# A state-space model and a dilated local attention on one core: the attention weights transposed by two DMAs instead of by TensorE

## The chip, the cores and the metric

The kernel runs on 1 core of one Trainium2 chip. The metric is the device time of one execution in microseconds (us), lower is better; the time before is the median of three runs. The engines are called TensorE (PE in the profile), VectorE (DVE), ScalarE (ACT), GpSimd (POOL) and SyncE (SP); SP issues nearly all DMAs of this kernel from one queue.

## The reference

Two layers over a sequence of 2048 rows of 448 values, joined along the last axis. Part A is a diagonal complex state-space model (448 states), a skip term added. Part B is attention with 16 heads of 28, in which each position sees itself and seven earlier ones, two steps apart (the eight taps).

```python
def A(x, ...):                       # x: 1 x 2048 x 448
    Lam_bar = exp(dt * Lam)          # dt = exp(log_dt)
    Bu = einsum("bld,pd->blp", x, ((Lam_bar - 1) / Lam)[:, None] * Bmat)
    for t in range(L):
        h = Lam_bar * h + Bu[:, t]
        hs.append(h)
    return 2 * einsum("blp,dp->bld", stack(hs, 1), Cmat).real + x * Dskip

def B(x, wqkv, wo):                  # H = 16, Dh = 28, W = 8, dil = 2
    q, k, v = split(x @ wqkv)
    idx = pos[:, None] - 2 * arange(8)[None, :]      # masked where idx < 0
    logits = einsum("bhsd,bhswd->bhsw", q, k[idx]) * Dh ** -0.5
    attn = softmax(where(idx >= 0, logits, -1e9), axis=-1)
    o = einsum("bhsw,bhswd->bhsd", attn, v[idx])
    return o.reshape(B, S, D) @ wo
```

## The kernel before

The sequence is cut into 128 chunks of 16 positions. A chunk is a partition (or a column, where a tensor is transposed), and the position in the chunk, j = 0 to 15, is a loop. Positions are taken in two halves (b = 1: j 8 to 15; b = 0: j 0 to 7) and each half in two groups of four (r = 1, 0; g = 2b + r).

**Units and their order.** Each piece of work is a unit, added to a planner (`P.add`) with its engine, its function and what it depends on. A unit's number is the order in which it was added. The list `ORDER` says in which order the units are issued; each engine, and each DMA queue, works through its own part of it strictly in turn, so an instruction that waits holds back all that stand behind it on the same engine. Where a unit may run on ScalarE or on VectorE (evictions of PSUM and a few copies), 1000 added to its number means VectorE. PSUM is given out as one double bank ("W") and six single ones ("s"); a unit that needs one waits until an eviction has released it.

**Projections (0 to 45 us).** SP loads x transposed by DMA (`load(j)`, L362), four positions to a group. TensorE forms q, k (L477, L484, L510) and v (L756, L763); ScalarE and VectorE evict them (L215 to L221, the helper `copy`). Units 46, 47 and 48 (`cx.double`, L450) copy 64 rows of the x of positions 8 to 11, 4 to 7 and 0 to 3 into the other 64, for matmuls of 64 rows (`rr`); each must wait for the four loads of its group.

**Logits.** `prod` (L650, L652, L656) multiplies q with shifted k on VectorE, two taps at a time (tp = 3, 2, 1, 0); products of tp 1 and 0 carry 1024 further elements (the last 64 feature rows, of two other taps). `summ` (L667, L673) sums over the features of a head with selector matmuls into the logits tile: its partitions are (i, r, h), the position in its group, the group and the head; its columns are eight rows, one for each tap, of the 128 chunks.

**Softmax.** `softmax(b)` adds eight units: mask; the maximum over the taps on VectorE (`top`, L696); its subtraction by matmul (`sub`, L700); the exponential on ScalarE (`exp`, L706); the sum by matmul (`tot`, L711); reciprocal and product on VectorE (`norm`, L715, L717), which leave the weights `attn_t` in the shape of the logits; eight transposes on TensorE into PSUM (`tr`, L723), one for each tap, after which a chunk is a partition; and two copies on ScalarE into `attn` (`ev`, L728), which reorder them for the value products. Units 206 to 213 are these for b = 1, 214 to 221 for b = 0.

**Values and output of part B.** `pv` multiplies the weights with the values on VectorE (`mul`, L818: 3584 elements, two taps by four positions) and sums (L821, L830, L833). The sums are transposed by DMA (`trd`, L858) or, for the last group, on TensorE (L870), then go through the output weights (L886, L894, L901), are evicted and stored (L911). `halo` copies values from the chunk before (L776, L777).

**Part A.** B and C are loaded; C is transposed by one DMA (L1010) and first used by the y matmuls. `scan` runs, for seven blocks of states m, a chain of matmuls and ScalarE evictions with powers of the state matrix that VectorE builds (`powers`, L1183). `outputs` forms y from the states (L1431, L1435), and stores it (L1450).

Of the kernel before, what the change touches and what calls it, by code (L numbers as in the profile page):

```python
# [88 lines left out]
def act(n):  # L89
    return n / 1200.0 + 0.055  # L90
# [115 lines left out]
class Ctx:  # L206
# [41 lines left out]
    def consts2(self):  # L248
# [22 lines left out]
        def masks():  # L271
            G.memset(mrow[:], 0.0)
            G.affine_select(out=mrow[:], in_=mrow[:], compare_op=ALU.not_equal, fill=-1e9,
                            base=-3, pattern=[[1, 4]], channel_multiplier=1)
            G.memset(mcol[:], 1.0)
            for b in range(2):
                for k in range(2):
# [39 lines left out]
class PartB:  # L317
# [372 lines left out]
    def softmax(self, b, prio):  # L690
# [29 lines left out]
        def tr():  # L720
            pt = box["pt"] = self.psum.tile([NCH, W, 2, 4, H], bf16, name="pt_at", tag="s")
            for w in range(W):
                nc.tensor.transpose(pt[:, w].rearrange("q r i h -> q i r h"), box["a"][:, w, :], cx.ident[:])  # L723
# [848 lines left out]
```

## Time and profile before

| | |
|---|---|
| median of three runs | 139.52 us (139.02 to 140.0) |
| the profiled execution | 138.77 us |
| its span, first to last instruction | 137.1 us |
| granted TensorE clock | 1.000 |
| busy, share of the span: TensorE | 130.8 us, 95% |
| VectorE | 124.1 us, 91% |
| ScalarE | 89.9 us, 66% |
| GpSimd | 17.3 us, 13% |

The profile shows one execution. A busy TensorE is not TensorE at its peak: matmuls overlap, and their ends are modelled. A group line reads: code line, engine, operation, output<-input with shapes, count, then busy us, mean ns of one, and the engine's idle time ahead of them with what ended it. A timeline line begins with its start and its length; a line with SPq shows SP issuing a DMA. The chain of waits follows the last instruction back to what released it, step by step. A row by stage gives a window, its width, and for PE, PEld (weight loads), DVE, ACT and POOL the busy time with the number of instructions; then the clock, the DMA engines' busy share and GB/s.

### The profile page before, as it was taken

To read this page: it belongs to the slowest core of one execution; us is meant where nothing else is said; L and a number is where in the kernel's file an instruction comes from. 1 tells how busy PE (TensorE), PEld (TensorE's weight loads), DVE (VectorE), ACT (ScalarE), POOL (GpSimd) and SP (SyncE) were. 2 spreads that over 40 slices of the span, in tenths; PEclk is the share of its full clock that TensorE was granted. 3 is DMA by queue.
4 is the path that set the end of the run, shared out by engine and by line. 5 is a ranking of instruction groups with operands and counts; after the bars stand their busy time and mean duration, and the time that the engine had idled before them with its cause. 6 is when DMAs were issued, how large, how long until landed. Compare 5 with 4: busy or idle time off the path is not lost.

```text
span 137.1 us, 2853 instructions
## 1 busy us (share of the span) xinstructions
PE 130.8 (95%) x1078; PEld 68.1 (50%) x1085; DVE 124.1 (91%) x136; ACT 89.9 (66%) x202; POOL 17.3 (13%) x69
## 2 busy tenths in 40 slices
PE   5999999999999999999999999999999999999990
PEld 1534334444556453756534663554665555445750
DVE  2369999899999999999999999999999999999950
ACT  3555588998553977856685999987737252463571
POOL 7589800028000000000000000000000000000000
PEclk9999999999999999999999999999999999999999
DMA  4988944554643938835899009600000464917654
GB/s 130 263 135 199 190 88 60 153 117 112 82 100 67 104 69 134 154 77 154 235 155 244 6 0 106 200 0 2 0 5 0 120 148 42 245 49 237 197 167 140
DMA packets 39582, 16.05 MB, mean 117 GB/s; under 512 B 31573, under 2 KB 38932, under 8 KB 39569
## 3 DMA queue, kind: packets, MB, share of 16 engines
q1 hardware_dynamic: 39506, 15.87, 54.5%
q8 instruction: 8, 0.13, 0.4%
q14 instruction: 5, 0.04, 0.1%
q10 hardware_dynamic: 63, 0.01, 0.0%
HBM read 4.32 MB, written 3.67 MB: 58 GB/s over the span
## 4 chain that ended last, share of the span: by engine, by line
PE 81%; SPq 10%; ACT 3%; DMA 2%; issue 1%; ACTq 0%
PE y_ps L1435 16%; PE v_ps L763 7%; SPq L362 6%; PE qk_ps L477 6%; PE scb L1233 6%; PE wo_ps L894 5%; PE scp L1233 5%; PE logits L667 4%; DMA rb<-in_B_x_dram 2%; PE wo_ps L901 2%; PE scb L1292 2%; PE scP L1233 2%; PE scb L1257 2%; PE y_ps L1431 2%; PE v_ps L756 2%
## 5 line engine op out<-in xcount | busy, mean ns | idle before, releaser
L818 DVE TENSOR_TENSOR prods<-attn,vd 128x3584 bf16<-128x3584 bf16 x12 | 24.0, 2017 | 0.0
L821 DVE TENSOR_TENSOR rb<-rb,prods 128x3584 bf16<-128x3584 bf16 x11 | 22.2, 2019 | 0.1
L652 DVE TENSOR_TENSOR prods<-qk 128x3072 bf16<-128x3072 bf16 (+1 forms) x15 | 19.1, 1325 | 0.0
L1435 PE MATMUL y_ps<-Ccat,qk 128*128 128x448 bf16 x60 | 15.1, 352 | 0.1
L477 PE MATMUL qk_ps<-rb 128*128 128x512 bf16 x60 | 14.4, 379 | 0.5 <-DMA rb<-in_B_x_dram 0.3
L215 ACT CAST qk<-wo_ps 128x448 bf16<-128x448 f32 (+1 forms) x16 | 8.2, 528 | 10.1 <-PE wo_ps L894 6.5
L215 ACT CAST vd<-v_ps 128x448 bf16<-128x448 f32 x15 | 7.4, 539 | 5.8 <-PE v_ps L763 4.5
L1435 PE MATMUL y_ps<-Ccat,h 128*128 128x448 bf16 x45 | 11.0, 353 | 0.0
L1233 PE MATMUL scb<-xaT_sb,Bcat 128*128 128x512 bf16 x42 | 10.9, 380 | 0.0
L1233 PEld LDWEIGHTS <-Bcat 128*128 128x128 bf16 x84 | 7.6, 100 | 6.6 <-issue 0.4
L1285 ACT CAST ubuf<-scb 128x64 bf16<-128x64 f32 x35 | 7.1, 218 | 5.6 <-PE scb L1292 3.5
L763 PE MATMUL v_ps<-rb 128*128 128x448 bf16 x48 | 9.9, 353 | 0.0
L217 ACT ACTIVATE qk<-qk_ps 64x512 bf16<-64x512 f32 (+1 forms) x15 | 8.9, 599 | 0.9 <-PE qk_ps L484 0.4
L656 DVE TENSOR_TENSOR prods<-qk 128x768 bf16<-128x768 bf16 (+3 forms) x18 | 9.1, 565 | 0.3 <-ACT qk L215 0.2
L477 PEld LDWEIGHTS <-rb 128*128 128x128 bf16 x60 | 5.6, 98 | 7.6 <-issue 0.7
L1435 PEld LDWEIGHTS <-qk 128*128 128x128 bf16 x60 | 5.9, 98 | 5.3
L818 DVE TENSOR_TENSOR rb<-attn,vd 128x3584 bf16<-128x3584 bf16 x4 | 8.1, 2020 | 0.1
L894 PE MATMUL wo_ps<-wo_p,rb 128*128 128x448 bf16 x36 | 8.1, 354 | 0.0
L215 ACT CAST qk<-qk_ps 128x512 bf16<-128x512 f32 (+2 forms) x11 | 6.3, 585 | 2.7 <-DVE qk L219 1.2
L1183 DVE TENSOR_TENSOR pw<-Dm,spair 128x1920 bf16<-128x1920 bf16 x7 | 8.1, 1150 | 0.0
L1233 PE MATMUL scp<-xaT_sb,Bcat 128*128 128x512 bf16 x30 | 7.8, 380 | 0.0
L667 PE MATMUL logits<-prods,Zsel 128*32 128x256 bf16 x192 | 7.4, 274 | 0.0
(199 smaller groups left out, 260.9 us busy)
## 6 DMA issues: line engine op xcount, KB each, us to landing
out_dram<-qk SPq DMA_DIRECT2D x32, 112.0 KB, 1.8
vd<-vd SPq DMA_DIRECT2D x3, 392.0 KB, 4.4
rb<-in_B_wqkv_dram SPq DMA_DIRECT2D x3, 336.0 KB, 4.6
qk<-in_A_x_dram SPq DMA_DIRECT2D x1, 448.0 KB, 4.2
ra<-in_A_B_re_dram SPq DMA_DIRECT2D x1, 392.0 KB, 4.4
ra<-in_A_B_im_dram SPq DMA_DIRECT2D x1, 392.0 KB, 5.7
rb<-in_A_C_re_dram SPq DMA_DIRECT2D x4, 98.0 KB, 2.8
rb<-in_A_C_im_dram SPq DMA_DIRECT2D x4, 98.0 KB, 3.1
```

Of the source, the lines that this page charges most:

```text
L215: nc.scalar.copy(out, in_)
L217: nc.scalar.mul(out, in_, scale)
L477: nc.tensor.matmul(out(n), lhsT=w(n, full, k), rhs=self.xT[:, j:j + 4, k, :], start=(not rfirst and k == 1), stop=(rfirst and k == KT - 1) ...
L652: V.tensor_tensor(out.rearrange("p i j k q -> p i (j k) q"), qq.unsqueeze(1).to_broadcast([NCH, 2, 4 * nk, NCH]), bass.AP(kk.tensor, kk.of ...
L656: V.tensor_tensor(jk(out[:, i, a:e]), qq, kk, op=ALU.mult)
L667: nc.tensor.matmul(lg[32 * i:32 * i + 32, 2 * tp:2 * tp + 2, :], lhsT=cx.Z[:, kt, zs], rhs=pr[:, :, i, kt, :], start=(new and kt == 0), st ...
L763: nc.tensor.matmul(box["ps"][:].rearrange("p h d -> p (h d)"), lhsT=self.xT[:, j, k, :], rhs=self.wv[:, k, :], start=False, stop=(k == KT ...
L818: V.tensor_tensor(tmp[i].rearrange("p (j d h) -> p j d h", j=8, d=DH), aa, self.vd[:, o:o + 8], op=ALU.mult)
L821: V.tensor_tensor(acc, acc, tmp[i], op=ALU.add)
L894: nc.tensor.matmul(ps[:], lhsT=self.oTd[g][:, a + kt], rhs=self.wo_p[:, 5 * e + kt, :], start=False, stop=(kt == 2), skip_group_check=True)
L1233: mt(box[i], lhsT=self.Bcat[:, k, m, :], rhs=self.xk(slice(i, None, 4), k), start=(i % 2 == 0 and k == 0), stop=False, **kw)
L1435: nc.tensor.matmul(ps, lhsT=h, rhs=self.Ccat[:, m, :], start=(m == 0 and not skip), stop=(m == NM - 1), skip_group_check=True)
```

## The change

`tr` and `ev` go; in their place the unit `turn` issues one DMA transpose on SP's queue for each half, from `attn_t` in SBUF straight to `attn` in SBUF. The DMA leaves (i, r, h) and the taps in the order in which they stand in the logits tile. So the logits matmuls now write the two taps of a pair two rows apart, such that taps that are used together by one value product are neighbours; the mask's row is laid out to match, and `mul` reads its weights with other strides. The softmax has seven units for each half instead of eight: after the change the first turn is unit 212 and the second 219, and numbers behind 213 are lower by one, those behind 221 by two.

`ORDER` is another list throughout. Its beginning, which holds the places named below, and the stretches with the two turns:

```diff
 ORDER = [
-    1, 22, 4, 5, 2, 3, 0, 36, 38, 40, 24, 41, 39, 7, 8, 6, 9, 19, 13, 12, 11, 10, 14, 15, 18, 16, 17, 1037, 26,
-    28, 45, 1043, 49, 50, 67, 62, 63, 44, 1042, 30, 1068, 51, 64, 54, 21, 29, 31, 35, 32, 222, 1052, 1066, 55,
-    1058, 1053, 56, 1057, 1065, 1046, 82, 83, 69, 70, 84, 71, 171, 1085, 1072, 59, 60, 61, 74, 75, 76, 87, 73,
-    78, 79, 88, 47, 1086, 1077, 172, 181, 223, 33, 262, 80, 154, 81, 103, 104, 90, 91, 105, 92, 95, 173, 107,
...
+    0, 22, 1, 36, 1037, 2, 38, 39, 4, 21, 5, 40, 45, 41, 24, 26, 28, 3, 49, 50, 30, 43, 62, 63, 29, 8, 44, 64,
+    65, 51, 1042, 54, 1052, 55, 6, 7, 67, 1053, 9, 69, 1046, 56, 70, 71, 66, 1068, 11, 35, 1058, 31, 74, 73, 19,
+    12, 75, 76, 1059, 1057, 171, 78, 1060, 13, 1079, 1080, 10, 1047, 32, 1081, 77, 87, 1088, 72, 82, 61, 83, 84,
...
+    302, 304, 279, 198, 246, 247, 201, 303, 203, 199, 213, 529, 280, 281, 338, 248, 282, 283, 530, 249, 253,
+    255, 284, 285, 257, 528, 214, 250, 251, 286, 252, 215, 305, 307, 287, 216, 531, 288, 254, 292, 533, 306,
...
+    395, 396, 565, 569, 570, 423, 424, 425, 450, 397, 566, 218, 219, 538, 539, 540, 571, 572, 426, 427, 451,
...
```

In VectorE's own queue the first evictions and doubling copies run, before: 68, 52, 66, 58, 53, 57, 65, 46; after: 52, 53, 46, 68, 58, 59, 57, then the product 171, 60, 79, 80, 47. In front of the maximum of b = 1 stands, before, the product of b = 0, group 1, tp 3 (3072 elements); after, that of tp 1 (3072 and 1024). The reciprocal and product of b = 0 stand, before, ahead of the four value steps of group 2; after, behind the first of them. SP's queue behind the loads of x has, before: load of C, load of the output weights, a halo copy, their swap, the skip vector, two halo copies, the transpose of C, a halo copy, the first `trd`; after: the skip vector, a halo copy, the first turn, three halo copies, load of the output weights, load of C, the swap, the first `trd`, the transpose of C, a row of the skip term, one output store, the second turn.

The rest of the diff:

```diff
         def masks():
             G.memset(mrow[:], 0.0)
-            G.affine_select(out=mrow[:], in_=mrow[:], compare_op=ALU.not_equal, fill=-1e9,
-                            base=-3, pattern=[[1, 4]], channel_multiplier=1)
+            v = mrow[:].rearrange("p (z y) -> p y z", z=2)
+            G.affine_select(out=v, in_=v, compare_op=ALU.not_equal, fill=-1e9,
+                            base=-3, pattern=[[2, 2], [1, 2]], channel_multiplier=1)
...
+                    at = lambda t, i: lg[32 * i:32 * i + 32, 4 * (t // 2) + t % 2:4 * (t // 2) + t % 2 + 3:2, :]
                     for kt in range(3):
                         for i in range(4):
-                            nc.tensor.matmul(lg[32 * i:32 * i + 32, 2 * tp:2 * tp + 2, :],
+                            nc.tensor.matmul(at(tp, i),
                                              lhsT=cx.Z[:, kt, zs], rhs=pr[:, :, i, kt, :],
...
-        def tr():
-            pt = box["pt"] = self.psum.tile([NCH, W, 2, 4, H], bf16, name="pt_at", tag="s")
-            for w in range(W):
-                nc.tensor.transpose(pt[:, w].rearrange("q r i h -> q i r h"), box["a"][:, w, :], cx.ident[:])
-
-        def ev():
-            at = self.attn[b] = pool.tile([NCH, W // 2, 2, 2, 4, H], bf16, name="attn%d" % b)
-            for x in range(2):
-                nc.scalar.copy(at[:, 2 * x:2 * x + 2].rearrange("q z r y i h -> q y (z r) (i h)"),
-                               box["pt"][:, 4 * x:4 * x + 4].rearrange("q (y z) r i h -> q y (z r) (i h)", y=2))
+        def turn():
+            at = self.attn[b] = pool.tile([NCH, W, 4, 2, H], bf16, name="attn%d" % b)
+            nc.sync.dma_start(at[:].rearrange("q w i r h -> q w (i r h)"), box["a"][:].rearrange("p w q -> p (w q)"), transpose=True)
...
-        u = P.add("PE", pe(8, 128), tr, [u], -1, acq="s", rel="at")
-        self.u_attn[b] = P.add("ACT", 2 * act(512), ev, [u], -1, rel="s")
+        self.u_attn[b] = P.add("SP", 1.3, turn, [u], -1, rel="at", lat=3.0)
...
-                        aa = self.attn[b][:, 2 * (u // 4) + u % 2, r].rearrange("q y i h -> q (y i) h").unsqueeze(2).to_broadcast(
+                        w0 = 4 * (u // 4) + 2 * (u % 2)
+                        aa = self.attn[b][:, w0:w0 + 2, :, r, :].rearrange("q y i h -> q (y i) h").unsqueeze(2).to_broadcast(
                             [NCH, 8, DH, H])
```

More of the change, by code (lines that the diff above doesn't have):

```diff
@@ L672, in summ @@
                             for i in range(4):
-                                nc.tensor.matmul(lg[32 * i:32 * i + 32, 2 * t2:2 * t2 + 2, :],
+                                nc.tensor.matmul(at(t2, i),
                                                  lhsT=z, rhs=ub["p3"][:, :, i, 0, :],
```

54 rows, old and new, of the table ORDER are left out of this document.

## The prediction

> **What bounds the kernel now.** I read the page first (span, busy shares, chain of waits), then the busy time of each engine stage by stage, then VectorE's timeline where it ends.
>
> ```profile
> span 137.1 us, 2853 instructions
> PE 130.8 (95%) x1078; PEld 68.1 (50%) x1085; DVE 124.1 (91%) x136; ACT 89.9 (66%) x202; POOL 17.3 (13%) x69
> PE 81%; SPq 10%; ACT 3%; DMA 2%; issue 1%; ACTq 0%
> ...
> 10.00:18.00 8.00, 7.88 (x41) 3.07 (x40) 7.77 (x13) 4.23 (x9) 6.61 (x19) 1.00 0.96 176
> 18.00:30.00 12.00, 11.84 (x89) 5.79 (x90) 11.20 (x16) 11.39 (x22) 0.00 (x0) 1.00 0.53 112
> ...
> 75.00:90.00 15.00, 14.77 (x121) 8.43 (x124) 14.81 (x11) 13.88 (x42) 0.00 (x0) 1.00 0.40 77
> ...
> 105.00:120.00 15.00, 15.00 (x106) 8.25 (x104) 14.90 (x9) 6.24 (x12) 0.00 (x0) 1.00 0.59 128
> ...
> 126.36 2.09 DVE L833 TENSOR_TENSOR rb<-rb,prods 128x1792 bf16<-128x1792 bf16 x2
> ...
> 127.47 1.32 PE y_ps L1435 x7
> 128.79 1.34 PE pt_o L870 x24
> ```
>
> Two engines are full at once. In the rows by stage the first pair after the width is TensorE (PE), the second its weight loads, the third VectorE (DVE), the fourth ScalarE (ACT). In the rows shown VectorE is idle for 0.1 to 0.8 us of a stretch, TensorE for 0 to 0.2. The chain of waits names TensorE (81%), but the last lines show a tie: the last product of attention weights and values is summed on VectorE at 126.36 + 2.09 = 128.45, and TensorE takes the output transposes up at 128.79, straight from a y matmul. If only one of the two gets lighter, the other holds the end. ScalarE has room on the whole (66%) but not between 75 and 90 us (13.88 of 15).
>
> **What is removed.** Sixteen transposes on TensorE and four copies on ScalarE.
>
> ```profile
> 56.18 0.45 PE pt_at L723 x8
> 86.30 0.45 PE pt_at L723 x8
> ...
> L728 ACT COPY attn<-pt_at x4: 592/598/606, 56.8 to 87.7; 128x512 bf16<-128x512 bf16 x4
> ```
>
> TensorE: 2 x 0.45 = 0.9 us. Both groups lie on the chain, so I count them in full for TensorE. ScalarE: 4 x 0.598 = 2.4 us, half of it at 87 us, in the full stretch. A PSUM bank of six comes free earlier. VectorE loses nothing: its 80 planned units stay 80, and the evictions that change engine cancel (nine evictions and one doubling copy come to it, as many leave). So the busier claim of the tie is not touched by the removal itself.
>
> **What is added.** Two DMA transposes of 128x1024, eight blocks of 128x128 each, on SP's queue. The nearest rows are the transposes of the attention output (fourteen blocks, SBUF to SBUF, L858) and those of x (four blocks, from DRAM, L980).
>
> ```profile
> L858 SPq DMA_TRANSPOSE rb<-rb x3: 1511/1527/1561, 81.4 to 114.6; - x3
> DMA to landing us min/median/max: 4.0/4.0/4.0
> ...
> L980 SPq DMA_TRANSPOSE xaT_sb<-in_A_x_dram x15: 1259/1265/1983, 23.4 to 48.0; - x15
> DMA to landing us min/median/max: 2.5/2.8/4.6
> ...
> 49.93 1.23 DVE L717 TENSOR_TENSOR attn_t<-ex_sb,rsum 128x1024 bf16<-128x1024 bf16 x1
> 64.37 2.01 DVE L818 TENSOR_TENSOR rb<-attn,vd 128x3584 bf16<-128x3584 bf16 x1
> ...
> 82.53 1.23 DVE L717 TENSOR_TENSOR attn_t<-ex_sb,rsum 128x1024 bf16<-128x1024 bf16 x1
> 99.71 2.02 DVE L818 TENSOR_TENSOR rb<-attn,vd 128x3584 bf16<-128x3584 bf16 x1
> ```
>
> Eight blocks lie between: 1.3 to 1.5 us of issue, 2.8 to 4.0 us from issue to landing; I take 4.0, the SBUF row. What hides it is VectorE's own queue. For the first half of the positions (b=1), 64.37 - 51.16 = 13.2 us pass before between the normalised weights and their first use, and in the new order the same seven units stand between. One halo copy of the values stands right ahead of the turn; at as much issue as the turn itself it lands within about 6 us: hidden by 7. For b=0 the gap before is 99.71 - 83.76 = 15.9 us; in the new order the normalisation has moved one step back (behind the first two value products of the second group), and three steps remain between, mul and add, mul and add, add and half add:
>
> ```profile
> L818 DVE TENSOR_TENSOR prods<-attn,vd 128x3584 bf16<-128x3584 bf16 x12 | 24.0, 2017 | 0.0
> L821 DVE TENSOR_TENSOR rb<-rb,prods 128x3584 bf16<-128x3584 bf16 x11 | 22.2, 2019 | 0.1
> L830 DVE TENSOR_TENSOR rb<-rb 128x1792 bf16<-128x1792 bf16 x3 | 3.3, 1092 | 0.1
> L1183 DVE TENSOR_TENSOR pw<-Dm,spair 128x1920 bf16<-128x1920 bf16 x7 | 8.1, 1150 | 0.0
> ```
>
> That is 3 x 2.02 + 2 x 2.02 + 1.09 = 11.2 us of cover for 4.0 us: hidden by 7. Without the cover each would cost its 4.0 us. The Trainium skill speaks against the change: "VectorE: DVE Perf Modes", section The three transpose paths, gives 1309 ns for one 128x128 block by DMA and 390 ns on TensorE, and its rules say to use TensorE where PSUM will do. By that figure, one block after another, a turn would be an estimated 10.5 us; L858's row says 4.0 for fourteen blocks, 0.29 each, so the trace does not agree, and by either the turn still ends under its cover.
>
> **The layout.** The taps' new places change addresses alone: the logits matmuls write two runs of 128 apart from each other, which L1274 does already; both take 274 ns for 256 columns. The value product reads its weights in runs of 16 with a gap. That could cost at most what short runs cost elsewhere: L1183 reads runs of 2 and takes 1150 ns for 1920 elements, L818 2017 for 3584, the line through both being 0.52 ns per element and 0.15 us, so 0, and no gain is to be had either.
>
> ```profile
> L667 PE MATMUL logits<-prods,Zsel 128*32 128x256 bf16 x192 | 7.4, 274 | 0.0
> L1274 PE MATMUL scb<-eA,pw 128*128 128x256 bf16 x7 | 1.8, 274 | 0.1
> ```
>
> **SP's queue.** The two turns add about 2.8 us of issue. The loads of C and of the output weights go behind them and behind three halo copies; their order changes so that C's transpose now stands behind the first output transpose, which waits for the end of that group's sums on VectorE (81.4 before, the first start in L858's row). C's turned copy, whose issue to landing is the first line below, then lands near 81.4 + 1.6 + 6.7 = 90, against a first use at 97.41 in the second: 7 us spare.
>
> ```profile
> DMA to landing us min/median/max: 6.7/6.7/6.7
> ...
> 97.41 0.95 PE y_ps L1435 x5
> ```
>
> **The order of issue.** This is the larger part: I walked VectorE's new queue against the rows. Two places matter. (a) The doubling copy of x rows 8 to 11 (unit 46) is now third in the line of evictions, not eighth, and that of rows 4 to 7 (47) has come over from ScalarE.
>
> ```profile
> 9.73 0.68 DVE L221 TENSOR_SCALAR qk<-qk_ps 128x512 bf16<-128x512 f32 x1
> ...
> 14.47 0.29 DVE L219 COPY rb<-rb 64x512 bf16<-64x512 bf16 x1
> ...
> 4.02 5.21 SPq L362 DMA_TRANSPOSE rb<-in_B_x_dram  x4
> DMA to landing us min/median/max: 3.5/4.0/5.5
> 14.60 3.31 DMA rb<-in_B_x_dram
> ```
>
> The fourth load is issued at 4.02 + 3 x 1.3 = 7.9 and lands between 11.4 and 13.4, by the median 11.9. VectorE is there at 9.73 + 2 x 0.68 = 11.1, and by the median waits 0.8 us (0.3 to 2.3) with all its evictions, and with them TensorE's PSUM banks, behind it. The second copy is reached at 11.9 + 0.29 + 7 x 0.68 + 0.96 = 17.9 (seven evictions and one product later) with its load landing at 14.60 + 3.31 = 17.91, so it waits little. (b) Before the maximum of b=1 now stands another product of the next half, the one with the extra 1024 elements.
>
> ```profile
> L652 DVE TENSOR_TENSOR prods<-qk 128x3072 bf16<-128x3072 bf16 x9 | 15.7, 1751 | 0.0
> L652 DVE TENSOR_TENSOR prods<-qk 128x1024 bf16<-128x1024 bf16 x6 | 4.1, 685 | 0.0
> L650 DVE TENSOR_TENSOR prods<-qk 128x1536 bf16<-128x1536 bf16 x6 | 5.7, 962 | 0.7 <-ACT qk L215 0.5
> ...
> 43.23 1.72 PE v_ps L763 x9
> 44.95 0.43 PE logits L700 x2
> ```
>
> Before, TensorE subtracts the maximum (L700) the moment its three value groups end (43.23 + 1.72 = 44.95), with no slack. With the maximum 0.7 us later it waits 0.7 us; VectorE does not, it only does that work sooner.
>
> **The sum.** VectorE: +0.8 at (a), less the waits of 0.7 us ahead of L650 that the new places of those products let go: +0.1. TensorE: -0.9 for the transposes, +0.7 at (b), +0.3 inherited from (a) through PSUM: +0.1. ScalarE's 2.4 us help only where TensorE waits for it; the chain gives ScalarE 3% (4.1 us), and I credit 0.3. Together -0.2 us on a span of 137.1. The profiled execution took 138.77 us, 1.67 around its span, and lies 0.75 under the runs' median of 139.52; against the median I forecast 139.3. Its own bounds are -0.9 (the removal alone) and +1.9 (the 2.3 of (a) less what is credited): 138.6 to 141.4.
>
> **Rivals.** (1) The relief pays. TensorE gives back 0.9 and a quarter of the 4.1 us in which the chain waits for ScalarE, with VectorE's waits closing as well: 0.9 + 1.1 = 2.0 us, 137.5. For it: ScalarE at 13.88 of 15 where its copies go. Against: VectorE, whose work stays the same, would have to be 2 us earlier, and its idle time from 10 to 128 us is hardly that. (2) Slower: the front of VectorE's queue stands on the loads. If the fourth x load lands at the latest bound, the first copy waits 2.3 us and no later idle time absorbs it, since both engines are full from there on: 139.5 + 2.3 = 141.8. It decides above a landing of about 12.5. For: x loads saturate the DMAs (0.96 busy from 10 to 18). Against: the row's median. (3) Slower: the second turn stands on SP behind an output store of group 3, which waits for ScalarE. Before, SP stood 21.6 us behind such a store:
>
> ```profile
> SPq L1450 <- ACT qk L215: 24.5, 2, 21.6
> ```
>
> From 7 us of delay on, VectorE runs dry before the value products of b=0; with 3 us more, 142.5. Against: that store is the first to be ready. (4) The change does not do what it says, because the transposes were hidden: that is the forecast itself, in effect.
>
> **How the numbers follow.** Forecast 0.45, rival 1 0.22, rival 2 0.22, rival 3 0.11. The mild ends of rivals 2 and 3 stay within 1% (1.4 us, about what a measurement of this kernel can tell from no change); a few of the forecast's cases pass it on either side. So faster by over 1%: 0.24; within: 0.44; slower: 0.32. The range reaches a little past rivals 1 and 2, whose sizes are uncertain: 137.3 to 142.2.
>
> **What would show it.** Right: no TensorE or ScalarE instruction between L717 and the value products; VectorE without idle time before the first value products of b=0; VectorE's busy time within 0.5 us of 124.1; a wait of about 0.8 us ahead of the 64x512 copy at about 11 us; L700 late by under 1 us. Wrong: VectorE idle in the value stage, L818 slower than 2.02 us, the turns landing after 5 us, or the last sum on VectorE more than 1.5 us away from 128.45.

## The result, and the profile after

The changed kernel takes 141.03 us (median of 4 runs, 140.76 to 141.33) against 139.76 us for the kernel before in the same comparison (139.02 to 140.03): ratio 1.0121, 95% interval 1.0091 to 1.0152. It is slower by 1.2%, 1.3 us, beyond the 1% that the prediction took as the limit of a measurement. The forecast of 139.3 us ("no change") was wrong; the time lies inside its range, nearest to rival 2 (141.8), one of the two on the slow side.

The page after, span, busy shares and chain:

```profile
span 139.3 us, 2837 instructions
PE 131.8 (95%) x1069; PEld 67.8 (49%) x1069; DVE 124.6 (89%) x136; ACT 88.1 (63%) x198; POOL 17.4 (12%) x69
PE 74%; SPq 9%; DMA 6%; DVE 4%; ACT 2%; issue 2%; DVEq 0%; ACTq 0%
```

VectorE's busy time is what it was (124.6 against 124.1), ScalarE is 1.8 us lighter, and yet the span is 2.2 us longer. In the chain TensorE gives up seven points; DMA and VectorE gain eight, so there is new waiting. Busy time by stage (after TensorE's pair come weight loads, VectorE, ScalarE):

```profile
10.00:18.00 8.00, 8.00 (x40) 3.17 (x38) 7.35 (x11) 5.87 (x11) 7.16 (x20) 1.00 0.88 174
18.00:30.00 12.00, 10.56 (x69) 4.83 (x68) 11.13 (x16) 8.69 (x17) 0.33 (x1) 1.00 0.53 106
75.00:90.00 15.00, 14.66 (x114) 7.76 (x112) 14.83 (x12) 12.08 (x37) 0.00 (x0) 1.00 0.46 89
```

Between 18 and 30 us TensorE loses 1.28 us (11.84 before, 10.56 after), long before any attention weight exists. The relief of ScalarE shows where it was expected (12.08 instead of 13.88 from 75 to 90), but TensorE is no busier there. VectorE's and TensorE's timelines of that front:

```profile
10.01 1.29 DVE L219 CAST qk<-qk_ps 128x512 bf16<-128x512 f32 x2 [1.04 <-PE qk_ps L485]
11.33 0.29 DVE L219 COPY rb<-rb 64x512 bf16<-64x512 bf16 x1
...
17.08 0.68 DVE L221 TENSOR_SCALAR qk<-qk_ps 64x512 bf16<-64x512 f32 x1
18.58 0.29 DVE L219 COPY rb<-rb 64x512 bf16<-64x512 bf16 x1 [0.81 <-DMA rb<-in_B_x_dram]
...
21.21 0.62 DVE L1126 TENSOR_TENSOR Gd<-Dm,gs 128x896 bf16<-128x896 bf16 x1
```

```profile
18.63 0.37 PE L485 MATMUL qk_ps<-rb,wm 64*128 64x512 bf16 x1 [0.53 <-DMA rb<-in_B_x_dram]
...
21.98 0.61 PE L1162 MATMUL ps_b<-Gd,ra 128*128 128x128 bf16 x8 [0.62 <-DVE Gd L1126]
...
25.57 1.02 PE L511 MATMUL qk_ps<-rb 128*128 128x512 bf16 x4 [0.29 <-DVE qk L221]
...
132.55 0.92 PE L896 MATMUL wo_ps<-wo_p,rb 128*128 128x448 bf16 x4 [0.56 <-ACT qk L215]
```

The first doubling copy (x rows 8 to 11, at 11.33) does not wait. The second (rows 4 to 7) waits 0.81 us and starts at 18.58; TensorE waits for the same load, then for Gd (operands of the scan's setup), which is queued behind the copy, then for an eviction: 0.53 + 0.62 + 0.29 = 1.44 us. The last line is a wait at the other end, for ScalarE.

The timeline lists 2.40 us of TensorE's waits from its first projection on, against 0.44 before: these 1.44 in the front, 0.18 in the scan, 0.22 for the landing of group 3's outputs, and the 0.56 at the end. That is 1.96 us more, and from there on the execution is 1.94 us longer (table below), although 0.9 us of transposes are gone from it. So another 0.9 us went somewhere that no listed wait shows; where is open.

The turns themselves do what was forecast. SyncE's queue, the landing, and VectorE's first uses:

```profile
53.37 1.26 SPq L724 DMA_TRANSPOSE attn<-attn_t  x1
...
90.00 1.29 SPq L724 DMA_TRANSPOSE attn<-attn_t  x1
DMA to landing us min/median/max: 3.1/3.1/3.1
...
65.75 2.02 DVE L813 TENSOR_TENSOR rb<-attn,vd 128x3584 bf16<-128x3584 bf16 x1
...
100.93 2.02 DVE L813 TENSOR_TENSOR rb<-attn,vd 128x3584 bf16<-128x3584 bf16 x1
```

The turns land by about 56.5 and 93.1; both first uses start without a wait, 9 and 8 us later. The layout leaves the durations alone (L813 2.02 us; logits matmuls 274 ns as before).

### The profile page after: what moved, and what is told of

It is laid out like the page before. It is cut to its first block, busy times and chain, and to the rows that moved or that the text cites. A ratio compares the mean times of both kernels' runs of the same rounds, so it can differ in the third digit from the quotient of the medians.

```text
span 139.3 us, 2837 instructions
## 1 busy us (share of the span) xinstructions
PE 131.8 (95%) x1069; PEld 67.8 (49%) x1069; DVE 124.6 (89%) x136; ACT 88.1 (63%) x198; POOL 17.4 (12%) x69
## 4 chain that ended last, share of the span: by engine, by line
PE 74%; SPq 9%; DMA 6%; DVE 4%; ACT 2%; issue 2%; DVEq 0%; ACTq 0%
PE y_ps L1430 15%; PE v_ps L757 7%; SPq L363 6%; PE scb L1228 6%; PE wo_ps L889 5%; PE scp L1228 5%; PE logits L669 4%; DMA rb<-rb 3%; PE qk_ps L478 3%; DMA rb<-in_B_x_dram 3%; PE wo_ps L896 2%; PE scb L1287 2%; PE scb L1252 2%; PE y_ps L1426 2%; DVE qk L221 1%
## 5 line engine op out<-in xcount | busy, mean ns | idle before, releaser
L813 DVE TENSOR_TENSOR prods<-attn,vd 128x3584 bf16<-128x3584 bf16 x12 | 24.0, 2019 | 0.0
L1430 PE MATMUL y_ps<-Ccat,qk 128*128 128x448 bf16 x60 | 14.6, 352 | 0.0
L217 ACT ACTIVATE qk<-qk_ps 128x512 bf16<-128x512 f32 (+1 forms) x14 | 8.1, 596 | 5.7 <-PE qk_ps L485 3.1
L215 ACT CAST qk<-y_ps 128x448 bf16<-128x448 f32 (+1 forms) x9 | 5.9, 666 | 7.1 <-PE y_ps L1430 6.9
L215 ACT CAST qk<-qk_ps 128x512 bf16<-128x512 f32 (+1 forms) x12 | 6.8, 586 | 2.8 <-PE qk_ps L485 1.9
L813 DVE TENSOR_TENSOR rb<-attn,vd 128x3584 bf16<-128x3584 bf16 x4 | 8.1, 2020 | 0.1
```

Of the source, the lines that this page charges most:

```text
L215: nc.scalar.copy(out, in_)
L217: nc.scalar.mul(out, in_, scale)
L813: V.tensor_tensor(tmp[i].rearrange("p (j d h) -> p j d h", j=8, d=DH), aa, self.vd[:, o:o + 8], op=ALU.mult)
L1430: nc.tensor.matmul(ps, lhsT=h, rhs=self.Ccat[:, m, :], start=(m == 0 and not skip), stop=(m == NM - 1), skip_group_check=True)
```

## The experiments

Each ratio is to the kernel before in the same comparison. Its median lay between 139.13 and 139.76 us in the six comparisons (139.52 in the first row is the one that the prediction started from), so medians of different rows should not be subtracted. Executions differ at their very start (last section), so beside the measured ratio I give a second figure: the span less the start of TensorE's first projection, both from the profiled execution. It is no exact correction, because the loads do not move with TensorE: who starts late waits less for them.

| kernel | median us | ratio to before, 95% interval | span - first projection = rest, us |
|---|---|---|---|
| before | 139.52 | | 137.1 - 6.34 = 130.76 |
| changed kernel | 141.03 | 1.0121 (1.0091 to 1.0152) | 139.3 - 6.60 = 132.70 |
| e1, turns, old order | 139.89 | 1.0053 (1.0024 to 1.0082) | 138.2 - 7.17 = 131.03 |
| e2, old code, new order | 143.28 | 1.0271 (1.0223 to 1.0319) | 141.6 - 6.39 = 135.21 |
| h1, old front | 140.56 | 1.0074 (1.0038 to 1.0111) | 138.9 - 6.94 = 131.96 |
| t1, y 14 earlier | 141.44 | 1.0147 (1.0099 to 1.0194) | 139.9 - 7.22 = 132.68 |
| n1, no turning, new layout | 139.54 | 1.0035 (1.0015 to 1.0055) | 138.4 - 6.54 = 131.86 |
| n0, no turning, old layout | 139.71 | 1.0036 (1.0012 to 1.0061) | 137.7 - 7.05 = 130.65 |
| l1, layout alone | 139.50 | 1.0020 (0.9993 to 1.0046) | 137.6 - 7.18 = 130.42 |
| h2, old code, new front | 141.14 | 1.0135 (1.0111 to 1.0159) | 139.6 - 7.21 = 132.39 |
| f1, turns, new front alone | 141.55 | 1.0129 (1.0107 to 1.0151) | 139.6 - 6.47 = 133.13 |
| ht2, old front and end | 140.47 | 1.0093 (1.0071 to 1.0115) | 138.3 - 6.43 = 131.87 |
| mx, as ht2, maximum earlier | 140.31 | 1.0067 (1.0041 to 1.0094) | 138.7 - 6.58 = 132.12 |
| m1, copy 47 on ScalarE | 143.32 | 1.0255 (1.0205 to 1.0304) | 140.0 - 6.45 = 133.55 |
| m2, Gd ahead of copy 47 | 140.70 | 1.0115 (1.0070 to 1.0160) | 139.2 - 7.08 = 132.12 |
| m4, x row 4 earlier | 141.20 | 1.0129 (1.0088 to 1.0170) | 139.6 - 7.26 = 132.34 |
| m6, both | 141.02 | 1.0113 (1.0081 to 1.0144) | 138.8 - 6.25 = 132.55 |
| e1b, second turn late | 150.00 | 1.0772 (1.0748 to 1.0795) | 148.3 - 7.17 = 141.13 |
| p2, late matmuls out | 138.86 | 0.9979 (0.9955 to 1.0002) | 136.8 - 6.83 = 129.97 |
| pv2, late work out on both | 138.33 | 0.9915 (0.9881 to 0.9949) | 136.8 - 6.55 = 130.25 |

**The turns without the new order (e1), the new order without the turns (e2).**

```diff
 ORDER: that of before; transposes (212, 220) and copies (213, 221) drop out
+ SP: load of C, turn of b=1, loads of the output weights, ...
+ SP: ..., skip loads, turn of b=0, y stores
```

> The changed code (turns by DMA, taps in the new order) in the old order of issue: the first turn stands on SP's queue behind the load of C, the second behind the last loads and ahead of the y stores. Theory O (the order of issue costs the 1.3 us, above all VectorE's copy of x rows 4 to 7 standing on its load at the front, and the y matmuls of position block 14 left to the very end; the turns and the layout cost nothing): between 138.8 and 139.8 us, ratio to before 0.993 to 1.000. Rival T (the turns or the layout cost it, by a way the trace does not show as a wait): 140.6 to 141.2, ratio 1.006 or more. Rival R (the relief of TensorE and ScalarE pays once the order is out of the way): 138.0 or less.

```diff
 ORDER: that of the changed kernel, on the old code
+ the transposes of b=0 right behind their normalisation, its copies behind them
```

> The old code (16 transposes on TensorE, four copies on ScalarE, old layout) in the new order of issue; the transposes and copies stand right behind the normalisations they belong to, as near as that order allows. Theory O: 141.0 to 142.0 us, ratio to before 1.009 to 1.016, at or above the changed kernel, since it keeps the new order and has TensorE's 0.9 us besides. Rival T: 139.5 to 140.0, ratio about 1.000.

The new code in the old order costs 0.5%, by its interval 0.2 to 0.8%: somewhat under half of the loss, at most two thirds. That is slower than theory O allowed and just under the 1.006 at which T begins, so this run does not decide between them. In e2 the new order alone is far slower than expected, 2.7%. Its profile has two waits of TensorE that the changed kernel has not: 0.52 us for a copy of the scan, and 2.03 us (0.22 in the changed kernel) for the output transposes of group 3, which landed 6.03 us after their issue, where the changed kernel shows 4.24 in the same place of the queue. So e2 says that the order costs, not how much.

**Is the removal worth anything (n1, n0, l1)?**

```diff
 def norm():      # n1, on e1; n0 does the same in the old layout
-    box["a"] = pool.tile([NCH, W, NCH], bf16, name="attn_t", ...)
+    at = self.attn[b] = pool.tile([NCH, W, 4, 2, H], bf16, ...)   # written here, not turned
 def turn():
-    nc.sync.dma_start(at[...], box["a"][...], transpose=True)
+    pass
```

> The changed kernel in the old order of issue with the turning left out altogether: no transposes on TensorE, no copies on ScalarE, no DMA turns; the value products read weights that are not turned. Theory W (the 16 transposes stood in stretches in which TensorE waits for ScalarE's copies in the scan in any case, so that their 0.9 us turn into waiting): 139.1 to 139.7 us, ratio to before 0.998 to 1.003, and TensorE waits 0.3 us for the copy of ubuf right where the first transposes were. Rival R (the relief is worth 0.9 us or more as my prediction counted it): 138.5 or less, ratio 0.994 or less. Rival T (the DMA turns themselves cost what the turns in the old order lost): this kernel at before's time and 0.4 us or more below the turns in the old order.

> The kernel before with the turning left out (no transposes, no copies of them; the value products read weights that are not turned), old layout, old order. If the removal alone is worth nothing because TensorE then waits where the transposes stood (0.30 us for ubuf near 57, 0.45 ahead of L886 near 87): ratio 0.998 to 1.002. If the removal by itself costs what the same kernel in the new layout lost: 1.003 or more. If relief pays: 0.994 or less.

> The kernel before with the taps' new layout alone: mask, two runs of 128 in the logits matmuls, weights read by the value products in the new places; transposes on TensorE, copies on ScalarE (in the new order of elements) and order of issue as before. Layout free: 139.0 to 139.5 us, ratio 0.998 to 1.002. Layout costs (the rival for the 0.35% that the kernel without any turning lost in the old order): ratio 1.003 or more.

Leaving the turning out altogether, by any engine, gains nothing: 1.0035 and 1.0036, in both layouts (n1's profiled execution has a wait of 0.57 us for a load of the scan's x that n0's has not, hence its longer rest). Rival R falls. T has no support, as e1 with its turns and n1 without any differ by less than their intervals, and the layout alone (l1) cannot be told from no change. TensorE's timelines show where the 0.9 us went. Before, then e1, then n0:

```profile
56.02 0.61 PE L723 MATMUL pt_at<-ident,attn_t 128*128 128x128 bf16 x8
...
86.13 0.61 PE L723 MATMUL pt_at<-ident,attn_t 128*128 128x128 bf16 x8
86.89 0.36 PE L886 MATMUL wo_ps<-wo_p,rb 64*128 64x448 bf16 x2
```

```profile
57.25 0.22 PE L1283 MATMUL scb<-ubuf,pw 128*128 128x64 bf16 x1 [0.30 <-ACT ubuf L1280]
...
87.25 0.38 PE L1259 MATMUL scb<-e,pw 128*128 128x512 bf16 x1 [0.19 <-ACT e L1256]
87.90 0.36 PE L881 MATMUL wo_ps<-wo_p,rb 64*128 64x448 bf16 x2 [0.27 <-DMA rb<-rb]
```

```profile
56.89 0.22 PE L1284 MATMUL scb<-ubuf,pw 128*128 128x64 bf16 x1 [0.30 <-ACT ubuf L1281]
...
86.89 0.38 PE L1260 MATMUL scb<-e,pw 128*128 128x512 bf16 x1 [0.19 <-ACT e L1257]
87.55 0.36 PE L882 MATMUL wo_ps<-wo_p,rb 64*128 64x448 bf16 x2 [0.28 <-DMA rb<-rb]
```

The transposes stood in gaps of the scan, in which TensorE waits for ScalarE's small copies, and ahead of a matmul that cannot start before the output transposes of group 3 have landed. Take 0.45 us out at 86 and 0.19 + 0.27 = 0.46 us of waiting comes in; take 0.45 out at 56 and 0.30 comes back at once. In n0 the three waits make 0.77 of the 0.90 us, which leaves 0.13, and from the first projection on its profiled execution is 0.11 us shorter than that of before (130.65 and 130.76). That by the measured ratio a kernel which only does less is still 0.35% slower, above what either forecast had for "worth nothing" (1.002 and 1.003), I cannot explain; it is less than the 0.45% between the medians of before in different comparisons.

**Where in the order: front and end (h1, t1, ht2, mx).**

```diff
 # h1: units of the front (loads, projections, setup, first products), then the rest
-ORDER = front of the changed kernel + rest of the changed kernel
+ORDER = front of before + rest of the changed kernel
```

> The changed kernel with only its front (loads of x, projections, setup and the first products of the logits) put back into the old order; the rest, the tail with it, stays. Theory O puts the larger part of the loss there (TensorE is 1.6 us behind by 26 us): 139.8 to 140.3 us, ratio to before 1.000 to 1.004, and TensorE no longer waits for the copy near 18.6 us. Rival S (slack later gives the front back, as TensorE's lag shrinks from 1.6 to 0.9 us by 90 us): the end moves by 0.3 us or less, 140.7 to 141.0. Rival T: 141.0.

```diff
 # t1, TensorE (y n: y matmuls of position n; wo: output weights; pt_o: last
 # output transposes); the add of y 14 on VectorE moves forward with it
-y 12, wo 8, y 13, y 15, pt_o 0, 1, 2, wo 0, 1, 2, pt_o 3, y 14, wo 3
+y 14, y 12, wo 8, y 13, y 15, pt_o 0, 1, 2, wo 0, 1, 2, pt_o 3, wo 3
```

> The changed kernel with only the last y sums mended: the seven matmuls of position block 14 go back ahead of those of blocks 12 and 13 and ahead of the last output transposes. Theory O: TensorE's stretch from the last output transposes to the end shrinks from 7.0 us by the 1.3 of the seven matmuls less what they take elsewhere, 140.1 to 140.6 us, ratio 1.003 to 1.006. Rival F (all of the loss is the front, the tail only waits for it): 140.9 to 141.1.

```diff
 # ht2: h1, and from the first y matmul on the order of before
-ORDER = front of before + rest of the changed kernel
+ORDER = front of before + middle of the changed kernel + end of before
```

> The changed kernel with its front, and everything from the first y matmul on, in the old order; the middle (softmax, scan, value projections, first value products) in the new one. Theory O (front about 0.7 us, end about 1.0 us, the middle nothing that lasts): 139.2 to 139.8 us, ratio to before 0.999 to 1.004. Rival M (the middle's later maximum, 0.6 us of waiting on TensorE, is kept to the end): 140.2 to 140.6, ratio 1.006 to 1.009.

```diff
 # mx: ht2, VectorE
-product tp=1 (3072 + 1024 elements), maximum of b=1, ..., product tp=3
+product tp=3 (3072 elements), maximum of b=1, ..., product tp=1
```

> As the kernel with front and end in the old order, with two products of the second half changed about on VectorE, so that the one of 3072 elements stands ahead of the maximum of b=1 and the one with 1024 more behind it. Theory B (the middle's 0.59 us wait of TensorE at the subtraction of the maximum is what that kernel keeps): the wait goes to 0.1 or less and the time comes down by 0.4 to 0.7 us, to 139.8 to 140.1, ratio 1.004 to 1.007. Rival G (the 0.59 us are taken up by the landing of group 3's turned copy near 85 us, which TensorE waits for in any case): 140.4 to 140.6, ratio 1.009.

The old front brings back about half a per cent (1.0121 to 1.0074, with intervals that overlap a little), less than theory O said and more than rival S. It uncovers the wait that step (b) of the prediction had named:

```profile
46.27 0.59 PE L702 MATMUL logits<-mx,nident 128*128 128x512 bf16 x2 [0.59 <-DVE mx L698]
```

With the products changed about (mx) this wait is gone from the timeline; 1.0093 becomes 1.0067, but the intervals overlap, so its worth is unsettled. mx's profiled execution is not the shorter one, as it has a wait of 0.80 us in the front, where ht2's has 0.30:

```profile
18.79 2.75 PE L478 MATMUL qk_ps<-rb 128*128 128x512 bf16 x12 [0.80 <-ACT qk L217]
```

The end was my second suspect, since the seven matmuls of y 14 had moved to the very end, with the wait of 0.56 us before them. No gain shows there. t1 and ht2 are no faster than the kernels that they mend (1.0147 against 1.0121, 1.0093 against 1.0074), though ht2 has no wait at the end; both miss theory O. In t1 the 0.56 us are gone, but the work that came forward left waits of 0.15 and 0.73 us behind, and the execution from the first projection on is as long as the changed kernel's (132.68 and 132.70):

```profile
135.65 0.93 PE L896 MATMUL wo_ps<-wo_p,rb 128*128 128x448 bf16 x4 [0.73 <-ACT rb L870]
```

**The front by itself (h2, f1).**

```diff
 # h2 on the old code, f1 on the changed code
-ORDER = front of before + rest of before
+ORDER = front of the changed kernel + rest of before
```

> The kernel before, transposes on TensorE and old layout, with the front alone in the new order (loads of x, projections, setup, first products of the logits); the rest in the old order. Theory O (the front order costs by itself, with no turn involved): 0.5 to 1.2 us slower, ratio 1.004 to 1.009, and TensorE waits for the copy of x rows 4 to 7 and for Gd between 18 and 26 us as in the changed kernel. Rival S (waits of the old order further back swallow it): ratio under 1.002.

> The changed code (turns by DMA, new layout) with the front alone in the new order and the rest in the old one. Theory H (the holes on TensorE that the removed transposes leave, 0.30 us near 57 and 0.46 near 87 us, swallow half of the front's 1.6 us): the turns in the old order plus 0.8 us, ratio to before about 1.010. Rival D (VectorE comes out of the front 1.6 us late as well, so its sums and the landing that TensorE waits for near 87 us come as much later): the front's delay passes whole, 140.9 us or more, ratio 1.013 to 1.017.

This shows that the front costs by itself. On the old code, with no DMA turn in it, its new order costs 1.35%, as much as the whole change. On the new code it is to be counted against e1, the same code in the old order: 1.0129 against 1.0053, 0.76% (0.4 to 1.1% by both intervals); h1, which takes it out again, gave 0.47%, hardly more than its noise. So in the changed kernel the front is about half of the loss or somewhat more. The other half per cent is there without it, in e1, and most of that in n0 and n1 as well, unexplained. The rest of the new order adds nothing on the new code (1.0121 with it, 1.0129 without), but on the old code e2 is 1.3% behind h2. Rival S falls. Between theory H and rival D the times do not decide: f1 is at the lower bound of D, but the 0.76% against e1 are about 1.1 us, between H's 0.8 and D's 1.6. D's mechanism does show in the traces. TensorE waits in h2 for Gd as in the changed kernel (the row names a DMA, but VectorE's Gd ended at 21.54 + 0.62 = 22.16, just before), and SyncE's rows show that VectorE, too, leaves the front late: the output transposes of group 3 are issued when its sums end. First h2's TensorE and VectorE, then the issue in before, h2 and f1:

```profile
22.31 0.61 PE L1167 MATMUL ps_b<-Gd,ra 128*128 128x128 bf16 x8 [0.62 <-DMA rb<-in_B_x_dram]
...
25.91 1.02 PE L510 MATMUL qk_ps<-rb 128*128 128x512 bf16 x4 [0.29 <-DVE qk L221]
```

```profile
21.54 0.62 DVE L1131 TENSOR_TENSOR Gd<-Dm,gs 128x896 bf16<-128x896 bf16 x1
```

```profile
81.45 1.56 SPq L858 DMA_TRANSPOSE rb<-rb  x1
```

```profile
83.91 1.56 SPq L858 DMA_TRANSPOSE rb<-rb  x1
```

```profile
83.58 1.54 SPq L853 DMA_TRANSPOSE rb<-rb  x1
```

Counted from the first projection these are 75.11, 76.70 and 77.11 us: 1.6 and 2.0 us later, on an engine that is busy nearly throughout (91% of the span before).

**One wait, or the order as a whole (m1, m2, m4, m6)?**

```diff
-..., 1079, 1080, 10, 1047, 32, 1081, ..., 85, 174, 33, 154, ...
+..., 1079, 1080, 10, 47, 32, 1081, ..., 85, 174, 33, 154, ...         # m1: 47 on ScalarE
+..., 1079, 1080, 10, 32, 33, 1047, 1081, ..., 85, 174, 154, ...       # m2: 33 is Gd
 # m4: the loads of B (19) behind x row 4 (10) on SyncE; m6: m2 and m4
-SP: 11, 19, 12, 13, 10, 14
+SP: 11, 12, 13, 10, 19, 14
```

> The changed kernel with one unit alone moved: the doubling copy of x rows 4 to 7 runs on ScalarE again, as before, not on VectorE; every order as in the changed kernel. Theory V (VectorE's standing on that copy's load, 0.81 us, holds the evictions and the setup of Gd behind it): the waits of TensorE for Gd (0.62) and for the next eviction (0.29) go, 140.2 to 140.6 us, ratio 1.005 to 1.008. Rival L (TensorE needs those x rows at that place in any case and waits for the load itself): 140.9 to 141.1, ratio 1.011 or more.

> The changed kernel with one unit moved on VectorE: Gd (0.62 us) stands ahead of the doubling copy of x rows 4 to 7, in the stretch in which VectorE waits for that copy's load, not four units behind it. Theory V (what is queued behind that wait costs, Gd above all): TensorE's wait for Gd (0.62) goes, 140.3 to 140.7 us, ratio to before 1.007 to 1.010. Rival P (the order of TensorE's bands against the loads holds the front, Gd only shows it): the wait moves to the next operand, 140.9 to 141.2, ratio 1.012.

> The changed kernel with one unit moved on SyncE: the loads of the scan's B (0.66 and 0.63 us of issue) go behind the load of x row 4, not ahead of rows 6, 7 and 4, so that this row lands 1.3 us earlier. Theory V: VectorE's wait of 0.81 us at the copy and TensorE's of 0.53 behind it go; 140.0 to 140.5 us, ratio 1.005 to 1.009. Rival P: 140.9 or more. What could go wrong in both: B comes 4 us later, and TensorE waits for it at its first use near 22 us.

> The changed kernel with both moves, B's loads behind x row 4 and Gd ahead of the copy. Theory V: the front is mended, as with the old front, 139.8 to 140.5 us, ratio 1.003 to 1.008. Rival P: ratio 1.010 or more.

None is measurably faster than the changed kernel. m1 (1.0255) and m6 (1.0081 to 1.0144, if barely) lie outside what theory V forecast, so V fell; the intervals of m2 and m4 alone would still let it stand. What TensorE waits for in the front, in m1, m2, m4 and m6:

```profile
19.68 0.81 PE L478 MATMUL qk_ps<-rb 128*128 128x512 bf16 x3 [2.71 <-ACT qk L215]
```

```profile
19.42 0.39 PE L485 MATMUL qk_ps<-rb 64*128 64x512 bf16 x1 [0.57 <-DVE rb L219]
...
25.53 1.02 PE L511 MATMUL qk_ps<-rb 128*128 128x512 bf16 x4 [0.53 <-DVE qk L221]
```

```profile
19.20 0.39 PE L485 MATMUL qk_ps<-rb 64*128 64x512 bf16 x1 [0.16 <-DVE rb L219]
22.25 0.61 PE L1162 MATMUL ps_b<-Gd,ra 128*128 128x128 bf16 x8 [0.62 <-DVE Gd L1126]
25.85 1.02 PE L511 MATMUL qk_ps<-rb 128*128 128x512 bf16 x4 [0.29 <-DVE qk L221]
```

```profile
18.93 0.39 PE L485 MATMUL qk_ps<-rb 64*128 64x512 bf16 x1 [0.99 <-DVE rb L219]
25.05 1.02 PE L511 MATMUL qk_ps<-rb 128*128 128x512 bf16 x4 [0.18 <-DVE qk L221]
```

The waits add up to 1.44 us in the changed kernel, 1.10 in m2, 1.07 in m4 and 1.17 in m6. But a late start alone lowers this sum. t1 has the changed kernel's front, starts its first projection 0.62 us later, and waits 0.62 + 0.29 = 0.91 us; no wait for the load is listed there:

```profile
18.84 0.37 PE L485 MATMUL qk_ps<-rb,wm 64*128 64x512 bf16 x1
22.21 0.61 PE L1162 MATMUL ps_b<-Gd,ra 128*128 128x128 bf16 x8 [0.62 <-DVE Gd L1126]
25.81 1.02 PE L511 MATMUL qk_ps<-rb 128*128 128x512 bf16 x4 [0.29 <-DVE qk L221]
```

So m2 and m4, which start late too (7.08 and 7.26), have gained nothing that shows: in m2 the mended wait for Gd comes back at the copy and at the eviction. m6 starts early (6.25) and waits less than f1, whose front is the changed kernel's (6.47; 0.68 + 0.62 + 0.29 = 1.59); its time shows no gain beyond the noise. m1 is the worst, as ScalarE now stands on the load with its evictions behind it (its profiled execution, 141.79 us, is one of its fastest). What is left of the explanation, that TensorE's bands as a whole are laid badly against the operands, is argued and not shown: no run here put one band back by itself, so which of them is open.

**The second turn behind an output store (e1b), and relief behind 87 us (p2, pv2).**

```diff
 # e1b, SP, from e1
-skip loads, turn of b=0, store of y 5
+skip loads, store of y 5, turn of b=0
```

> The changed code in the old order of issue, with the second turn behind the first output store on SP's queue instead of right behind the loads that follow the output transposes of group 3. Theory K (two DMA transposes in flight slow each other, which made group 3's landing 5.6 us instead of 4.0 and TensorE wait 0.27 us): the landing is back near 4.0, that wait is gone, 139.4 to 139.8 us, ratio 1.000 to 1.003. Rival Q (what the turns in the old order lose lies elsewhere): as there, ratio 1.005. In both the turned weights are there before their first use near 100 us.

```profile
107.57 0.35 SPq L1445 DMA_DIRECT2D out_dram<-qk  x1
108.01 1.23 SPq L724 DMA_TRANSPOSE attn<-attn_t  x1
...
111.23 2.02 DVE L813 TENSOR_TENSOR rb<-attn,vd 128x3584 bf16<-128x3584 bf16 x1 [10.89 <-DMA out_dram<-qk]
```

Neither theory's number: the store waits for its y until 107.57, the turn behind it, and VectorE 10.89 us for the turn. This is the mechanism of the prediction's rival 3, at far more than its 142.5. In the changed kernel it does not occur: the store ahead of the second turn was issued at 89.54, the turn at 90.00. e1b also refutes theory K: group 3's landing took 5.59 us and kept TensorE waiting 0.23 us here with no turn in flight.

```diff
 # p2, output projection of positions 4 to 7
-for kt in range(3):
+for kt in range((2 if j == 4 else 1) if g == 1 else 0, 3):
 # pv2: p2 and, in the value sums
-add(n)
+if (b, r, n) != (0, 0, 2):
+    add(n)
```

> The kernel before with five matmuls of the output projection of positions 4 to 7 left out, 5 x 0.187 = 0.93 us of TensorE's work behind 100 us, as much as the 16 transposes have. Theory W (until 86.9 us the end is set by VectorE's sums, the landing of their turned copy and the scan's copies on ScalarE, from there on by TensorE alone; relief of TensorE pays only behind that point): 0.7 to 0.9 us faster, ratio to before 0.993 to 0.996. Rival V (VectorE holds the end, as a tie of the two would have it): no change, ratio 0.998 or more.

> The kernel before with the same five late matmuls left out as in the kernel with late work out, and one addition of VectorE's last value sums besides (2.02 us near 121). Theory E (behind 87 us TensorE and VectorE tie: 0.93 us off TensorE alone gave 0.58, the rest went into a wait of 0.35 for VectorE's last sum): that wait goes and the whole 0.93 us comes out, 138.2 to 138.5 us, ratio 0.992 to 0.995. Rival X (something else holds the end, the output transposes and ScalarE's copies): as without the addition left out, ratio 0.997 to 0.999.

```profile
128.71 1.18 PE L870 MATMUL pt_o<-ident,rb 128*128 128x128 bf16 x18 [0.35 <-DVE rb L833]
```

The same 0.93 us that were worth nothing at 56 and 86 bring at most little when they go late on TensorE alone: the medians are 0.58 us apart (139.44 to 138.86), but the ratio is 0.9979 with an interval that just includes 1, which misses theory W and is nearest to rival V. The row above shows what took part of it, a wait of TensorE for VectorE's last sum. With VectorE relieved as well this wait is gone and the ratio is 0.9915, which the whole 0.93 us (0.7%) fits and theory X does not. So the tie at the end that the prediction read from the page is there: relief of both engines behind 87 us pays.

## Why the prediction was wrong, point by point

- **The removal, -0.9 for TensorE "in full", and 0.3 credited to ScalarE**: this step failed. The transposes lay on the chain of waits, and still they only filled gaps that ScalarE's copies and a DMA landing set. Measured: no gain (n0, n1). Rival 4 ("hidden") had this right and was called "the forecast itself, in effect", yet the sum takes the 0.9 off. With both terms at 0 the sum reads +1.0 instead of -0.2, near the measured 1.3; that nearness is luck, as the next steps show.
- **The turns, 1.3 to 1.5 us of issue, 2.8 to 4.0 of landing, hidden by 7 us**: right (1.3, 3.1, hidden by 8 to 9). The estimate of 10.5 us by the Trainium skill's 1309 ns a block ("VectorE: DVE Perf Modes", The three transpose paths) does not hold here: 3.1 us for eight blocks.
- **The layout, 0**: right within what l1 can show.
- **Step (a), the x copies, +0.1 in the sum for VectorE and +0.3 for TensorE**: this is the other term that failed. The place was right, the front of the queues. But the first copy did not wait: VectorE reached it at 11.33, near the 11.1 reckoned, and the load was there, earlier than the 11.4 to 13.4 reckoned. The second, dismissed with "it waits little", waited 0.81: VectorE was ready at 17.08 + 0.68 = 17.76, but the load came at 18.58, not at 17.91. And the price was read off one queue. Of TensorE's 1.44 us only the 0.29 for an eviction is what the 0.3 stood for; the 0.53 for the load and the 0.62 for Gd were not in the sum. TensorE loses 1.28 us between 18 and 30, and VectorE's sums come 1.6 us later in h2. In time the front costs 1.35% on the old code and 0.76% on the new.
- **Step (b), the maximum later by 0.7**: the wait came out at 0.59 where it shows (h1); in the changed kernel no wait shows there, where TensorE arrives late itself. So in the changed kernel the term is 0.
- **Rival 2 (141.8, slower, VectorE's front on the x loads)** came nearest in the number, with the place right, but not by its mechanism: the copy that it names did not wait at all, and mending the wait of the next one (m2, m4, m6) does not mend the time.
- **The last sum within 1.5 us of 128.45**: it ends at 127.59 + 2.10 = 129.69, 1.24 later; the test was too wide to show the loss.

## What to carry to other kernels

A full engine on the chain of waits does not make each of its instructions worth their time: ask what the next instruction on that engine waits for, and take an instruction's removal as gain only if that operand is already there. When an order of issue is shifted "a little" around a change, price the shift on all queues together, first where the loads come in, and measure it alone: the old code with one stretch of the new order is the run to make, and a run on the new code is to be counted against the new code in the old order. A transfer moved behind another on a queue is only as early as the one ahead of it.

## What was not expected of the hardware

TensorE's first matmuls take nearly twice as long in some executions as in others, and the moment at which they become fast differs between kernels that start alike. The groups of three 512-column matmuls ahead of the first projection, in before and in e1:

```profile
5.33 0.82 PE L303 MATMUL warm_ps<-prods 128*128 128x512 bf16 x3
```

```profile
5.92 1.46 PE L304 MATMUL warm_ps<-prods 128*128 128x512 bf16 x3
```

Same work, 0.82 and 1.46 us, though the granted clock reads 1.00 in both; the first projection begins at 6.34 and 7.17, and between 6.25 and 7.26 over all the kernels here. The Trainium skill ("TensorE: Matmul & The Clock Gate", Part 1: The HAM clock gate) says that the change hangs on a free-running activity window that does not reset when a kernel starts; the trace agrees in that the moment varies. Here this is up to 1 us, as much as most of the effects above, so single profiles were compared from the first projection on.

DMA transposes of the same shape do not land in the same time. Group 3's outputs, from issue to use in the chains of the changed kernel, e1 and e2:

```profile
81.76 4.24 DMA rb<-rb
```

```profile
82.22 5.64 DMA rb<-rb
```

```profile
82.10 6.03 DMA rb<-rb
```

In n0, f1 and e1b it is 5.59 to 5.68 us. TensorE waits on that landing, and no run here shows what sets it.
